# GELU on two hidden tiles at a time in a fused attention and MLP kernel

## The chip, the cores and the metric

The kernel runs on one core of a Trainium2 chip. The metric is device time in microseconds (us) of one execution; lower is better. Executions of the kernel before agree within 0.6% (421.8 to 424.2 us). Engines are named as in the profile: PE (matmul), PEld (its weight loads), DVE (vector), ACT (scalar), POOL, SP.

## The reference

Four layers are applied to x of 2048 rows by 512 columns, bf16: linear attention, MLP, attention, MLP, with the same weights twice. Cut to what matters:

```python
def _B_ref(x, w1, b1, w2, b2):                  # the MLP; F = 1792
    y = _layernorm(x, axis=-1)
    h = _gelu(jnp.einsum("bsd,df->bsf", y, w1) + b1)     # tanh form of GELU
    return jnp.einsum("bsf,fd->bsd", h, w2) + b2

x = x + _A_ref(_layernorm(x), A_wqkv, A_wo)     # linear attention, 32 heads of 16
x = x + _B_ref(_layernorm(x), B_w1, B_b1, B_w2, B_b2)
# ... and both once more
```

## The kernel before

All data stays on the core. Rows are worked in 4 chunks of 512. In an MLP layer PE makes h transposed, one tile of 128 hidden units by 512 rows at a time (4 matmuls, 14 tiles a chunk), and later y for each of 16 row tiles (15 matmuls; a y needs all 14 h tiles of its chunk). GELU of one h tile takes five instructions, on DVE and ACT in turn. A pipeline helper issues stage k of item i in step i+k, so that every engine has a fixed program order:

```python
for f in range(NF): H(0, f)                 # NF = 14
for c in range(1, NCH):
    ytiles = list(range(4 * (c - 1), 4 * c))
    for f in range(NF):
        H(c, f)
        if f in (5, 7, 9, 11) and ytiles:   # a y of the chunk before
            Y(ytiles.pop(0))
for t in range(4 * (NCH - 1), NT): Y(t)
# stages of an h item:
#  0 PE   4 matmuls into one of 8 PSUM banks
#  1 ACT (f % 3 == 1) or DVE: X = psum + b1        -> frees the bank
#  2 ACT  Q = Square(k * X)
#  3 DVE  P = (Q + c) * X                          (SCALAR_TENSOR_TENSOR, "STT")
#  4 ACT  S = Sigmoid(2 * P)
#  5 DVE  hT = S * X                               ("multiply")
# stages of a y item: 5 PE 15 matmuls; 8 DVE residual, then layer norm of the next layer is queued
_pipeline(items, 9, b_stage, per_step=lambda: K.drain(1))   # one queued piece of layer norm a step
```

PSUM banks are handed out in the order in which they were freed.

## Time and profile before

The median was 423.06 us in 6 runs.

| stage (from the trace of the kernel before) | us |
|---|---|
| first matmul | at 16.1 |
| attention, layer 1 | 87.1 |
| MLP, layer 2 | 118.6 |
| attention, layer 3 | 79.6 |
| MLP, layer 4, to the last matmul | 116.3 |

Each stage is counted from its own first matmul to the next stage's. First, groups of instructions of the kernel before: line, engine, operation, tiles, shapes and count; then busy time and mean ns of one; then idle time of the engine ahead of them, with what ended it.

```profile
L669 PE MATMUL ps<-lnT,w_sb 128*128 128x512 bf16 x448 | 108.3, 389 | 11.1 <-DVE st L681 8.3 <-ACT st L677 2.0 <-issue 0.6
L717 PE MATMUL ps<-w_sb,hT 128*128 128x512 bf16 x434 | 103.2, 387 | 7.0 <-ACT st L699 4.4 <-DVE hT L704 2.0
L693 DVE SCALAR_TENSOR_TENSOR st<-st 128x512 bf16<-128x512 bf16 x112 | 76.8, 686 | 6.7 <-ACT st L688 5.8
L699 ACT ACTIVATE st<-st 128x512 bf16<-128x512 bf16 x112 | 69.7, 622 | 17.4 <-DVE st L693 17.2
L681 DVE TENSOR_SCALAR st<-ps,b_f 128x512 bf16<-128x512 f32 x72 | 53.6, 745 | 7.2 <-PE ps L669 7.1
L704 DVE TENSOR_TENSOR hT<-st 128x512 bf16<-128x512 bf16 x112 | 45.7, 417 | 2.5 <-ACT st L699 2.5
L677 ACT ACTIVATE st<-ps,b_f 128x512 bf16<-128x512 f32 x40 | 26.8, 670 | 1.8 <-PE ps L669 1.8
```

L669 is h, L717 is y. PE waits 8.3 us in all for the DVE bias add (which frees its bank), and 4.4 + 2.0 us ahead of y for GELU results.

Next, windows of layer 2 in the same trace: a stretch of time, its length, busy us (and instructions) of PE, PEld, DVE, ACT, POOL, then the granted PE clock, the DMA share and GB/s.

```profile
112.00:116.00 4.00, 3.45 (x11) 1.20 (x12) 2.89 (x5) 3.63 (x5) 0.00 (x0) 0.72 0.70 131
124.00:128.00 4.00, 3.03 (x13) 0.95 (x12) 4.00 (x9) 3.81 (x8) 0.00 (x0) 1.00 0.02 4
128.00:132.00 4.00, 2.87 (x13) 0.86 (x11) 4.00 (x9) 3.78 (x8) 0.00 (x0) 1.00 0.00 0
132.00:136.00 4.00, 1.84 (x6) 0.68 (x6) 4.00 (x9) 3.90 (x8) 0.00 (x0) 0.78 0.00 0
136.00:140.00 4.00, 4.00 (x15) 1.49 (x14) 4.00 (x9) 3.54 (x7) 0.00 (x0) 0.79 0.00 0
160.00:172.00 12.00, 11.95 (x55) 5.04 (x55) 10.95 (x27) 8.39 (x16) 1.11 (x1) 1.00 0.23 44
```

Two regimes are seen. From 120 to 136 us DVE is always busy and PE is not: GELU sets the pace. From 160 us on PE is always busy: saving GELU time there buys nothing.

Last, PE's timeline in layer 2 of the same kernel (start, length, engine, line, operation, tiles, count, and in brackets the idle time before it and what ended it). First h, the last h before the first y, the first y, and the y of the last chunk:

```profile
103.12 7.07 PE L669 MATMUL ps<-lnT,w_sb 128*128 128x512 bf16 x32
131.62 1.02 PE L669 MATMUL ps<-lnT,w_sb 128*128 128x512 bf16 x4 [0.27 <-DVE st L681]
134.79 4.39 PE L717 MATMUL ps<-w_sb,hT 128*128 128x512 bf16 x13 [2.15 <-ACT st L699]
139.43 1.90 PE L669 MATMUL ps<-lnT,w_sb 128*128 128x512 bf16 x8
207.89 3.19 PE L717 MATMUL ps<-w_sb,hT 128*128 128x512 bf16 x14 [2.01 <-DVE hT L704]
```

The first y starts 31.7 us after the first h, and the y at 207.89 takes 3.19. (Some matmul records are missing from a trace, so 13 and 14 mean the same. Where it is the first of a y, the y seems to start about 0.2 us late and to take 2.97 us in place of 3.19; starts of a y are no better known than that.) The 2.01 us before the last chunk's y are a hole in the PE-bound part.

### The profile page before, as it was taken

The numbers are of one execution on the slowest core, as the hardware profiler recorded it, in microseconds if no ns is written. First come the engines' busy times: TensorE is split into PE (matmuls) and PEld (weight loads), VectorE is DVE, ScalarE is ACT, GpSimd is POOL, SyncE is SP. The second block draws the span as 40 slices with busy tenths as digits, with TensorE's granted clock in tenths as the row PEclk, the third lists the DMA queues.
The fourth block names the chain that finished last, engine by engine and source line by source line (L and its number), as shares of the span: only waits on it lengthen the run. The fifth ranks groups of instructions, "written<-read, shape, count | busy, mean of one in ns | idle before, by whom it ended". The sixth has DMA issues, their size and how long they took to land.

```text
span 420.4 us, 5871 instructions
## 1 busy us (share of the span) xinstructions
PE 363.6 (86%) x1921; PEld 164.4 (39%) x1952; DVE 338.7 (81%) x834; ACT 272.4 (65%) x524; POOL 24.9 (6%) x52
## 2 busy tenths in 40 slices
PE   0469997978776999999899999697887699999997
PEld 0124445544322444444344444654332244444442
DVE  4788776999699989999836877699879998987941
ACT  5536662545499896896727666255649987886820
POOL 6320000000100001000000000000100000000000
PEclk9989999899998999999999999899989899999999
DMA  8997000021600001102022000002250000010011
GB/s 295 205 295 156 2 0 2 2 51 30 120 2 0 0 2 24 27 2 50 2 50 50 2 0 0 2 3 51 51 100 2 1 12 27 12 39 12 26 39 37
DMA packets 40688, 18.74 MB, mean 45 GB/s; under 512 B 35473, under 2 KB 39570, under 8 KB 40658
## 3 DMA queue, kind: packets, MB, share of 16 engines
q1 hardware_dynamic: 39506, 12.59, 14.3%
q0 software_dynamic: 1152, 5.77, 4.1%
q8 instruction: 16, 0.26, 0.2%
q14 instruction: 14, 0.11, 0.1%
HBM read 7.87 MB, written 2.10 MB: 24 GB/s over the span
## 4 chain that ended last, share of the span: by engine, by line
issue 58%; PE 24%; DVE 8%; ACT 5%; POOL 4%; DMA 1%; POOLq 0%; DVEq 0%
PE ps L717 15%; PE ps L669 7%; POOL rs L364 3%; ACT st L688 2%; DVE st L388 2%; DVE st L693 2%; PE ps L719 2%; DVE st L681 1%; ACT st L699 1%; DVE ln_tok L375 1%; ACT st L677 1%; DMA x_sb<-in_A_x_dram 1%; DVE hT L704 1%; ACT st L338 1%; DVE x_sb L427 0%
## 5 line engine op out<-in xcount | busy, mean ns | idle before, releaser
L669 PE MATMUL ps<-lnT,w_sb 128*128 128x512 bf16 x448 | 108.3, 389 | 11.1 <-DVE st L681 8.3
L717 PE MATMUL ps<-w_sb,hT 128*128 128x512 bf16 x434 | 103.2, 387 | 7.0 <-ACT st L699 4.4
L693 DVE SCALAR_TENSOR_TENSOR st<-st 128x512 bf16<-128x512 bf16 x112 | 76.8, 686 | 6.7 <-ACT st L688 5.8
L688 ACT ACTIVATE st<-st 128x512 bf16<-128x512 bf16 x112 | 69.2, 623 | 19.5 <-DVE st L681 18.1
L699 ACT ACTIVATE st<-st 128x512 bf16<-128x512 bf16 x112 | 69.7, 622 | 17.4 <-DVE st L693 17.2
L669 PEld LDWEIGHTS ps<-lnT,w_sb 128*128 128x128 bf16 x448 | 40.9, 99 | 72.4 <-issue 13.0
L717 PEld LDWEIGHTS ps<-w_sb,hT 128*128 128x128 bf16 x448 | 43.8, 100 | 61.5 <-DVE hT L704 7.1
L475 PE MATMUL ps<-wqkv_sb,lnT 128*128 128x512 bf16 x249 | 57.3, 385 | 3.7 <-DVE pqT L509 3.4
L681 DVE TENSOR_SCALAR st<-ps,b_f 128x512 bf16<-128x512 f32 x72 | 53.6, 745 | 7.2 <-PE ps L669 7.1
L427 DVE SCALAR_TENSOR_TENSOR x_sb<-ps,x_sb 128x512 bf16<-128x512 f32 x64 | 43.3, 684 | 18.9 <-PE ps L719 18.3
L338 ACT ACTIVATE st<-x_sb 128x512 bf16<-128x512 bf16 x64 | 39.6, 620 | 20.9 <-DVE x_sb L427 15.4
L491 ACT ACTIVATE st<-ps 128x512 bf16<-128x512 f32 x64 | 37.8, 598 | 22.3 <-PE ps L475 9.2
L704 DVE TENSOR_TENSOR hT<-st 128x512 bf16<-128x512 bf16 x112 | 45.7, 417 | 2.5 <-ACT st L699 2.5
L462 PE MATMUL ps<-lnT,wqkv_sb 128*128 128x512 bf16 x128 | 31.7, 404 | 16.0 <-DMA lnT<-ln_tok 16.0
L598 ACT ACTIVATE oT<-ps 128x512 bf16<-128x512 bf16 x32 | 19.0, 593 | 39.5 <-PE ps L591 39.5
L475 PEld LDWEIGHTS ps<-wqkv_sb,lnT 128*128 128x128 bf16 x256 | 25.3, 99 | 34.8 <-DVE pqT L509 3.9
L609 PE MATMUL ps<-wo_sb,oT 128*128 128x512 bf16 x118 | 32.3, 388 | 4.8 <-DVE den_sb L573 2.9
L364 POOL TENSOR_TENSOR rs<-rs,neg_half 128x4 f32<-128x4 f32 x16 | 16.4, 1027 | 281.3 <-DVE rs L361 157.0
L375 DVE TENSOR_SCALAR ln_tok<-x_sb,mv,rs 128x512 bf16<-128x512 bf16 x64 | 22.7, 417 | 12.4 <-POOL rs L364 12.4
L677 ACT ACTIVATE st<-ps,b_f 128x512 bf16<-128x512 f32 x40 | 26.8, 670 | 1.8 <-PE ps L669 1.8
L497 DVE TENSOR_SCALAR st<-st 128x512 bf16<-128x512 bf16 x64 | 18.3, 287 | 11.0 <-ACT st L491 10.8
L462 PEld LDWEIGHTS ps<-lnT,wqkv_sb 128*128 128x128 bf16 x128 | 13.0, 103 | 33.0 <-issue 19.9
(55 smaller groups left out, 261.2 us busy)
## 6 DMA issues: line engine op xcount, KB each, us to landing
w_sb<-in_B_w_dram POOLq DMA_DIRECT2D x2, 1792.0 KB, 8.8
x_sb<-in_A_x_dram SPq DMA_DIRECT2D x4, 512.0 KB, 7.6
out_dram<-x_sb SPq DMA_DIRECT2D x16, 128.0 KB, 1.7
wqkv_sb<-in_A_wqkv_dram POOLq DMA_DIRECT2D x1, 1536.0 KB, 10.2
wo_sb<-in_A_wo_dram POOLq DMA_DIRECT2D x1, 512.0 KB, 4.7
lnT<-ln_tok SPq DMA_TRANSPOSE x16, 4.3
b_bf<-in_B_b_dram SPq DMA_DIRECT2D x1, 3.5 KB
biasblk<-in_B_b_dram SPq DMA_DIRECT2D x1, 1.0 KB
```

What stands on the lines that cost most here:

```text
L338: self.add(E_ACT, lambda e: e.activation(junk, x_t, ACT.Square, accum_out=self.ss[:, 1, t:t + 1]), reads=[("x", t)], writes=[("st", sJ), ( ...
L427: self.add(E_DVE, lambda e: e.scalar_tensor_tensor(out=x_t, in0=ps_ap, scalar=0.0, in1=x_t, op0=ALU.add, op1=ALU.add, accum_out=self.ss[:, ...
L462: ins = e.matmul(ps[:], K.wqkv_sb[:, gp, g * 128:(g + 1) * 128], K.lnT_ap(c)[:, :, gp, :], start=(gp == 0), stop=(gp == NG - 1))
L475: ins = e.matmul(ps[:], K.lnT_ap(c)[:, tl, gp, :], K.wqkv_sb[:, gp, col0:col0 + 512], start=(gp == 0), stop=(gp == NG - 1))
L491: K.add(E_ACT, lambda e: e.activation(stE, ps[:], ACT.Exp), reads=[("ps", it.b)], writes=[("st", it.sE)], name="phi_exp")
L669: ins = e.matmul(ps[:], K.w1_sb[:, gp, f * 128:(f + 1) * 128], K.lnT_ap(c)[:, :, gp, :], start=(gp == 0), stop=(gp == NG - 1))
L681: K.add(E_DVE, lambda e: e.tensor_scalar(stX, K.ps[it.b][:], K.b1_f[:, f:f + 1], None, op0=ALU.add), reads=[("ps", it.b), ("c", "b1f")], w ...
L688: K.add(E_ACT, lambda e: e.activation(stQ, stX, ACT.Square, scale=kq), reads=[("st", it.sX)], writes=[("st", it.sQ)], name="g_sq")
L693: K.add(E_DVE, lambda e: e.scalar_tensor_tensor(out=stP, in0=stQ, scalar=GELU_C, in1=stX, op0=ALU.add, op1=ALU.mult), reads=[("st", it.sQ) ...
L699: K.add(E_ACT, lambda e: e.activation(stS, stP, ACT.Sigmoid, scale=2.0), reads=[("st", it.sP)], writes=[("st", it.sS)], name="g_sig")
L704: K.add(E_DVE, lambda e: e.tensor_tensor(dest, stS, stX, ALU.mult), reads=[("st", it.sS), ("st", it.sX)], writes=[("hT", slot, f)], name=" ...
L717: ins = e.matmul(ps[:], K.hT[:, slot, f, tl * 128:(tl + 1) * 128], K.w2_sb[:, f, :], start=(f == 0), stop=False)
```

## The change

The intent is to pay the fixed cost of each GELU instruction once for two h tiles. An h item is now a pair; Square, STT, Sigmoid and multiply are 1024 wide; the bias add stays 512 wide (its bias differs and each tile has its own bank), one half on DVE and the other on ACT. Staging buffers come from a free list so that two neighbours can be had. The y items stand after pairs 3, 4, 5, 6 of a chunk. Cut to its core:

```diff
-        for f in range(NF):
-            H(0, f)
+        for j in range(NPAIR):
+            H(0, j)
         for c in range(1, NCH):
             ytiles = list(range(4 * (c - 1), 4 * c))
-            for f in range(NF):
-                H(c, f)
-                if f in (5, 7, 9, 11) and ytiles:
+            for j in range(NPAIR):
+                H(c, j)
+                if j in (3, 4, 5, 6) and ytiles:
                     Y(ytiles.pop(0))
 ...
                 elif k == 1:
-                    if f % 3 == 1:   # ACT ... else DVE
+                    it.sX = K.alloc_st(2)
+                    stX = K.st2ap(it.sX)
+                    K.add(E_DVE, ... tensor_scalar(stX[:, 0:512], K.ps[it.bA][:], b1 of f0 ...), name="g_x")
+                    K.add(E_ACT, ... activation(stX[:, 512:1024], K.ps[it.bB][:], ACT.Identity, b1 of f0+1 ...), name="g_xa")
 ...
                 elif k == 2:
-                    stX, stQ = K.st[:, it.sX, :], K.st[:, it.sQ, :]
+                    stX, stQ = K.st2ap(it.sX), K.st2ap(it.sQ)      # 1024 wide
                     K.add(E_ACT, lambda e: e.activation(stQ, stX, ACT.Square, scale=kq), ...)
 ...   # stages 3, 4, 5 in the same way
```

The rest of the diff (own junk buffers for the layer norm sums, four den buffers instead of 16, one constant sharing another's buffer, an unused option to normalize on ACT) does no different work.

More of the change, by code (lines that the diff above doesn't have):

```diff
@@ L21 @@
 DEBUG_INST_MAP = {}
+TEST_SEP_IDENT = False
 GELU_C = math.sqrt(2.0 / math.pi)
@@ L157, in __init__ @@
         self.sems = {}
-        self.rr_st = 0
         self.free_banks = deque(range(8))
@@ L177, in release_bank, with alloc_st, release_st, st1 @@
         self.free_banks.append(b)
-    def next_st(self):
-        s = self.rr_st
-        self.rr_st = (self.rr_st + 1) % self.NST
-        return s
+    def alloc_st(self, n=1):
+        free = self.st_free
+        if n == 1:
+            u = free.popleft()
+            return u
+        for u in list(free):
+            if u % 2 == 0 and (u + 1) in free:
+                free.remove(u)
+                free.remove(u + 1)
+                return u
+        raise AssertionError("staging pool: no free pair (restructure the pipeline)")
+    def release_st(self, u, n=1):
+        for k in range(n):
+            assert (u + k) not in self.st_free
+            self.st_free.append(u + k)
+    def st1(self, u):
+        return self.st[:, u, :]
+    def st2ap(self, u):
+        return self.st[:, u:u + 2, :].rearrange("p a k -> p (a k)")
     def dump(self, name, src_ap, reads):
@@ L203, in alloc @@
         nc, P, NT, NG, NF, S, D = self.nc, self.P, self.NT, self.NG, self.NF, self.S, self.D
-        self.NST = 24
+        self.NST = 26
         self.NLN = 8
@@ L220, in alloc @@
         self.st = self.sb("st", [P, self.NST, 512], BF16)
+        self.st_free = deque(range(self.NST))
+        self.junk_act = self.sb("junk_act", [P, 2, 512], BF16)
+        self.junk_dve = self.sb("junk_dve", [P, 2, 512], BF16)
         self.wqkv_sb = self.sb("wqkv_sb", [P, NG, 3 * D], BF16)
@@ L230, in alloc @@
         self.rs = self.sb("rs", [P, 2, NT], F32)
-        self.den_sb = self.sb("den_sb", [P, NT, 32], F32)
-        self.rden = self.sb("rden", [P, NT, 32], F32)
+        self.nmr = self.sb("nmr", [P, NT], F32)
+        self.NDS = 4
+        self.den_sb = self.sb("den_sb", [P, self.NDS, 32], F32)
+        self.rden = self.sb("rden", [P, self.NDS, 32], F32)
         self.z_sb = self.sb("z_sb", [P, NG], F32)
@@ L236, in alloc @@
         self.neg_half = self.sb("neg_half", [P, 1], F32)
+        self.eps_col = self.sb("eps_col", [P, 1], F32)
         self.maskf = self.sb("maskf", [P, 128], F32)
@@ L239, in alloc @@
         self.mask8f = self.sb("mask8f", [P, 8], F32)
-        self.identf = self.sb("identf", [P, 128], F32)
+        self.identf = self.sb("identf", [P, 128], F32) if TEST_SEP_IDENT else self.maskf
         self.ident = self.sb("ident", [P, 128], BF16)
@@ L296, in build_consts @@
         self.add(E_DVE, lambda e: e.memset(self.neg_half[:], -0.5), writes=[("c", "neg_half")], name="c_neghalf")
+        self.add(E_DVE, lambda e: e.memset(self.eps_col[:], 1e-6), writes=[("c", "eps")], name="c_eps")
         for t in range(self.NT):
@@ L312, in build_consts @@
                  reads=[("c", "maskf")], writes=[("c", "mask16")], name="c_mask16")
-        self.add(E_POOL, lambda e: e.memset(self.identf[:], 1.0), writes=[("c", "identf")], name="c_id0")
+        self.add(E_POOL, lambda e: e.memset(self.identf[:], 1.0), reads=[("c", "mask16")],
+                 writes=[("c", "identf"), ("c", "maskf")], name="c_id0")
         self.add(E_POOL, lambda e: e.affine_select(self.identf[:], self.identf[:], [[1, 128]], ALU.is_equal, 0.0,
@@ L325, in build_consts @@
                  reads=[("c", "mask8f")], writes=[("c", "mask8f")], name="c_mask8c")
-    def ln_sum_tile(self, t):
-        x_t = self.x_sb[:, t, :]
-        sJ = self.next_st()
-        junk = self.st[:, sJ, :]
-        self.add(E_ACT, lambda e: e.activation(junk, x_t, ACT.Identity, accum_out=self.ss[:, 0, t:t + 1]),
-                 reads=[("x", t)], writes=[("st", sJ), ("ss0", t)], name=f"sum{t}")
     def ln_sumsq_tile(self, t):
         x_t = self.x_sb[:, t, :]
-        sJ = self.next_st()
-        junk = self.st[:, sJ, :]
+        junk = self.junk_act[:, t % 2, :]
         self.add(E_ACT, lambda e: e.activation(junk, x_t, ACT.Square, accum_out=self.ss[:, 1, t:t + 1]),
-                 reads=[("x", t)], writes=[("st", sJ), ("ss1", t)], name=f"sumsq{t}")
+                 reads=[("x", t)], writes=[("junk_act", t % 2), ("ss1", t)], name=f"sumsq{t}")
     def ln_chunk_stats(self, c, double):
@@ L365, in ln_chunk_stats, with ln_chunk_norm @@
                  reads=[("rs0", c), ("c", "neg_half")], writes=[("rs", c)], name=f"rstd{c}")
-    def ln_chunk_norm(self, c, lngroup):
+    def ln_chunk_norm(self, c, lngroup, act_tiles=0):
         P = self.P
@@ L370, in ln_chunk_norm @@
         s0 = (c % 2) * 4
+        if act_tiles:
+            nmr4 = self.nmr[:, t0:t0 + 4]
+            self.add(E_DVE, lambda e: e.scalar_tensor_tensor(out=nmr4, in0=self.mv[:, t0:t0 + 4, 0], scalar=-1.0,
+                                                             in1=self.rs[:, 1, t0:t0 + 4], op0=ALU.mult,
+                                                             op1=ALU.mult),
+                     reads=[("mv", t) for t in range(t0, t0 + 4)] + [("rs", c)], writes=[("nmr", c)], name=f"nmr{c}")
         for i in range(4):
@@ L374, in ln_chunk_norm @@
             dst = self.ln_tok[:, s0 + i, :]
-            self.add(E_DVE, lambda e, dst=dst, x_t=x_t, t=t: e.tensor_scalar(
-                dst, x_t, self.mv[:, t, 0:1], self.rs[:, 1, t:t + 1], op0=ALU.subtract, op1=ALU.mult),
-                reads=[("x", t), ("mv", t), ("rs", c)], writes=[("lnk", s0 + i)], name=f"norm{t}")
+            if i < act_tiles:
+                self.add(E_ACT, lambda e, dst=dst, x_t=x_t, t=t: e.activation(
+                    dst, x_t, ACT.Identity, bias=self.nmr[:, t:t + 1], scale=self.rs[:, 1, t:t + 1]),
+                    reads=[("x", t), ("nmr", c), ("rs", c)], writes=[("lnk", s0 + i)], name=f"norma{t}")
+            else:
+                self.add(E_DVE, lambda e, dst=dst, x_t=x_t, t=t: e.tensor_scalar(
+                    dst, x_t, self.mv[:, t, 0:1], self.rs[:, 1, t:t + 1], op0=ALU.subtract, op1=ALU.mult),
+                    reads=[("x", t), ("mv", t), ("rs", c)], writes=[("lnk", s0 + i)], name=f"norm{t}")
         src = self.ln_tok[:, s0:s0 + 4, :]
@@ L385, in ln_sum_tile_dve @@
         x_t = self.x_sb[:, t, :]
-        sJ = self.next_st()
-        junk = self.st[:, sJ, :]
+        junk = self.junk_dve[:, t % 2, :]
         self.add(E_DVE, lambda e: e.tensor_scalar(junk, x_t, 1.0, 0.0, op0=ALU.mult, op1=ALU.add,
                                                   accum_out=self.ss[:, 0, t:t + 1]),
-                 reads=[("x", t)], writes=[("st", sJ), ("ss0", t)], name=f"sumd{t}")
+                 reads=[("x", t)], writes=[("junk_dve", t % 2), ("ss0", t)], name=f"sumd{t}")
     def emit_ln_layer0(self):
@@ L398, in emit_ln_layer0 @@
             self.ln_chunk_norm(c, self.ln_groups[0][c])
-            if c == 1:
+            last = self.NCH - 1
+            if c == min(1, last):
                 self.load_wo()
-            if c == 2:
+            if c == min(2, last):
                 self.load_w1()
-            if c == 3:
+            if c == min(3, last):
                 self.load_w2()
@@ L422, in post_residual @@
             self.defer(lambda c=c, nl=nl: self.ln_chunk_stats(c, self.layer_kinds[nl] == "B"))
-            self.defer(lambda c=c, nl=nl: self.ln_chunk_norm(c, self.ln_groups[nl][c]))
+            self.defer(lambda c=c, nl=nl: self.ln_chunk_norm(c, self.ln_groups[nl][c],
+                                                                 act_tiles=(0 if self.layer_kinds[nl] == "B" else 0)))
     def residual(self, t, bank_res, ps_ap, name):
@@ L488, in a1_stage @@
                 else:
-                    it.sE = K.next_st()
-                    stE = K.st[:, it.sE, :]
+                    it.sE = K.alloc_st()
+                    stE = K.st1(it.sE)
                     K.add(E_ACT, lambda e: e.activation(stE, ps[:], ACT.Exp), reads=[("ps", it.b)],
@@ L494, in a1_stage @@
                 if it.kind != "v":
-                    it.sE1 = K.next_st()
-                    stE, stE1 = K.st[:, it.sE, :], K.st[:, it.sE1, :]
+                    it.sE1 = K.alloc_st()
+                    stE, stE1 = K.st1(it.sE), K.st1(it.sE1)
                     K.add(E_DVE, lambda e: e.tensor_scalar(stE1, stE, 1.0, 1e-6, op0=ALU.min, op1=ALU.add),
                           reads=[("st", it.sE)], writes=[("st", it.sE1)], name="phi_e1")
+                    K.release_st(it.sE)
             elif k == 3:
@@ L501, in a1_stage @@
                     ps = K.ps[it.b]
-                    stE1 = K.st[:, it.sE1, :]
+                    stE1 = K.st1(it.sE1)
                     if it.kind == "q":
@@ L512, in a1_stage @@
                     K.release_bank(it.b)
+                    K.release_st(it.sE1)
         _pipeline(items, 4, a1_stage, per_step=lambda: K.drain(1))
@@ L571, in a3_stage @@
                 den_ps = K.ps[it.bt][:, 0:32]
-                dsb, rd = K.den_sb[:, t, :], K.rden[:, t, :]
+                ds = t % K.NDS
+                dsb, rd = K.den_sb[:, ds, :], K.rden[:, ds, :]
                 K.add(E_DVE, lambda e: e.tensor_scalar(dsb, den_ps, 1e-6, None, op0=ALU.add),
-                      reads=[("ps", it.bt)], writes=[("den", t)], name=f"dene{t}")
-                K.add(E_DVE, lambda e: e.reciprocal(rd, dsb), reads=[("den", t)], writes=[("rden", t)],
+                      reads=[("ps", it.bt)], writes=[("den", ds)], name=f"dene{t}")
+                K.add(E_DVE, lambda e: e.reciprocal(rd, dsb), reads=[("den", ds)], writes=[("rden", ds)],
                       name=f"rden{t}")
@@ L581, in a3_stage @@
                     rd.unsqueeze(2).to_broadcast([P, 32, 16]), ALU.mult),
-                    reads=[("ps", it.b), ("rden", t)], writes=[("otk", it.slot)], name=f"o{t}")
+                    reads=[("ps", it.b), ("rden", ds)], writes=[("otk", it.slot)], name=f"o{t}")
                 K.release_bank(it.b)
@@ L628, in layer_B @@
         kq = math.sqrt(GELU_C * GELU_A)
+        assert NF % 2 == 0
+        NPAIR = NF // 2
         class It:
@@ L633, in layer_B, with H @@
         items = []
-        def H(c, f):
+        def H(c, j):
             it = It()
-            it.kind, it.c, it.f = "h", c, f
+            it.kind, it.c, it.f0 = "h", c, 2 * j
             items.append(it)
@@ L656, in layer_B, with hgroup, fn @@
             Y(t)
+        def hgroup(ps, c, f):
+            def fn(e):
+                ins = None
+                for gp in range(NG):
+                    ins = e.matmul(ps[:], K.w1_sb[:, gp, f * 128:(f + 1) * 128],
+                                   K.lnT_ap(c)[:, :, gp, :], start=(gp == 0), stop=(gp == NG - 1))
+                return ins
+            return fn
         def b_stage(it, k):
             if it.kind == "h":
-                c, f = it.c, it.f
+                c, f0 = it.c, it.f0
@@ L661, in b_stage @@
                 slot = c % 2
                 if k == 0:
-                    it.b = K.alloc_bank()
-                    ps = K.ps[it.b]
-                    def fn(e):
-                        ins = None
-                        for gp in range(NG):
-                            ins = e.matmul(ps[:], K.w1_sb[:, gp, f * 128:(f + 1) * 128],
-                                           K.lnT_ap(c)[:, :, gp, :], start=(gp == 0), stop=(gp == NG - 1))
-                        return ins
-                    K.add(E_PE, fn, reads=[("w", "w1")] + K.lnT_res(c), writes=[("ps", it.b)], name=f"h{c}_{f}")
-                elif k == 1:
-                    it.sX = K.next_st()
-                    stX = K.st[:, it.sX, :]
-                    if f % 3 == 1:
-                        K.add(E_ACT, lambda e: e.activation(stX, K.ps[it.b][:], ACT.Identity,
-                                                            bias=K.b1_f[:, f:f + 1], scale=1.0),
-                              reads=[("ps", it.b), ("c", "b1f")], writes=[("st", it.sX)], name="g_xa")
-                    else:
-                        K.add(E_DVE, lambda e: e.tensor_scalar(stX, K.ps[it.b][:], K.b1_f[:, f:f + 1], None,
-                                                           op0=ALU.add),
-                              reads=[("ps", it.b), ("c", "b1f")], writes=[("st", it.sX)], name="g_x")
-                    K.release_bank(it.b)
@@ new lines, in b_stage @@
+                    it.bA = K.alloc_bank()
+                    it.bB = K.alloc_bank()
+                    K.add(E_PE, hgroup(K.ps[it.bA], c, f0), reads=[("w", "w1")] + K.lnT_res(c),
+                          writes=[("ps", it.bA)], name=f"h{c}_{f0}")
+                    K.add(E_PE, hgroup(K.ps[it.bB], c, f0 + 1), reads=[("w", "w1")] + K.lnT_res(c),
+                          writes=[("ps", it.bB)], name=f"h{c}_{f0 + 1}")
+                elif k == 1:
+                    it.sX = K.alloc_st(2)
+                    stX = K.st2ap(it.sX)
+                    K.add(E_DVE, lambda e: e.tensor_scalar(stX[:, 0:512], K.ps[it.bA][:], K.b1_f[:, f0:f0 + 1], None,
+                                                       op0=ALU.add),
+                          reads=[("ps", it.bA), ("c", "b1f")], writes=[("st", it.sX)], name="g_x")
+                    K.release_bank(it.bA)
+                    K.add(E_ACT, lambda e: e.activation(stX[:, 512:1024], K.ps[it.bB][:], ACT.Identity,
+                                                        bias=K.b1_f[:, f0 + 1:f0 + 2], scale=1.0),
+                          reads=[("ps", it.bB), ("c", "b1f")], writes=[("st", it.sX + 1)], name="g_xa")
+                    K.release_bank(it.bB)
@@ L685, in b_stage @@
                 elif k == 2:
-                    it.sQ = K.next_st()
-                    stX, stQ = K.st[:, it.sX, :], K.st[:, it.sQ, :]
+                    it.sQ = K.alloc_st(2)
+                    stX, stQ = K.st2ap(it.sX), K.st2ap(it.sQ)
                     K.add(E_ACT, lambda e: e.activation(stQ, stX, ACT.Square, scale=kq),
-                          reads=[("st", it.sX)], writes=[("st", it.sQ)], name="g_sq")
+                          reads=[("st", it.sX), ("st", it.sX + 1)],
+                          writes=[("st", it.sQ), ("st", it.sQ + 1)], name="g_sq")
@@ L690, in b_stage @@
                 elif k == 3:
-                    it.sP = K.next_st()
-                    stX, stQ, stP = K.st[:, it.sX, :], K.st[:, it.sQ, :], K.st[:, it.sP, :]
+                    it.sP = K.alloc_st(2)
+                    stX, stQ, stP = K.st2ap(it.sX), K.st2ap(it.sQ), K.st2ap(it.sP)
                     K.add(E_DVE, lambda e: e.scalar_tensor_tensor(out=stP, in0=stQ, scalar=GELU_C, in1=stX,
                                                                   op0=ALU.add, op1=ALU.mult),
-                          reads=[("st", it.sQ), ("st", it.sX)], writes=[("st", it.sP)], name="g_p")
+                          reads=[("st", it.sQ), ("st", it.sQ + 1), ("st", it.sX), ("st", it.sX + 1)],
+                          writes=[("st", it.sP), ("st", it.sP + 1)], name="g_p")
@@ L696, in b_stage @@
+                    K.release_st(it.sQ, 2)
                 elif k == 4:
-                    it.sS = K.next_st()
-                    stP, stS = K.st[:, it.sP, :], K.st[:, it.sS, :]
+                    it.sS = K.alloc_st(2)
+                    stP, stS = K.st2ap(it.sP), K.st2ap(it.sS)
                     K.add(E_ACT, lambda e: e.activation(stS, stP, ACT.Sigmoid, scale=2.0),
-                          reads=[("st", it.sP)], writes=[("st", it.sS)], name="g_sig")
+                          reads=[("st", it.sP), ("st", it.sP + 1)],
+                          writes=[("st", it.sS), ("st", it.sS + 1)], name="g_sig")
@@ L701, in b_stage @@
+                    K.release_st(it.sP, 2)
                 elif k == 5:
-                    stX, stS = K.st[:, it.sX, :], K.st[:, it.sS, :]
-                    dest = K.hT[:, slot, f, :]
+                    stX, stS = K.st2ap(it.sX), K.st2ap(it.sS)
+                    dest = K.hT[:, slot, f0:f0 + 2, :].rearrange("p f k -> p (f k)")
                     K.add(E_DVE, lambda e: e.tensor_tensor(dest, stS, stX, ALU.mult),
-                          reads=[("st", it.sS), ("st", it.sX)], writes=[("hT", slot, f)], name="g_out")
+                          reads=[("st", it.sS), ("st", it.sS + 1), ("st", it.sX), ("st", it.sX + 1)],
+                          writes=[("hT", slot, f0), ("hT", slot, f0 + 1)], name="g_out")
@@ L706, in b_stage @@
+                    K.release_st(it.sS, 2)
+                    K.release_st(it.sX, 2)
             else:
```

## The prediction

> **What bounds it now.** The page gives PE 86%, DVE 81%, ACT 65%. Windows over the two MLP layers show two regimes. (1) Start of the layer: in the timeline the first h matmul of layer 2 runs at 103.1 us, the first y matmul at 134.8 us. From 120 to 136 us DVE is busy 4.00 of every 4 us and ACT about 3.8, PE only 1.8 to 3.0: PE waits for PSUM banks that the bias add frees. Layer 4 repeats it (301 to 333 us). PE idles 8.5 us there in layer 2. (2) From the first y on, PE is busy 11.95 of 12 us, DVE about 11, ACT 8.4 to 11.4: PE-bound, so GELU work saved there is worth nothing. One hole remains: 2.0 us at 205.9 us in layer 2, where y of the last chunk waits for the last GELU output on DVE. Layer 4 has none.
>
> **What the change does.** GELU works on two 512-wide tiles at once: 56 wide Squares, Sigmoids, STTs and multiplies in place of 112 each; bias adds split evenly (DVE 72 to 56, ACT 40 to 56). The first y moves from after 23 h tiles in PE's order to after 26. The rest should cost nothing.
>
> **Costs.** Mean durations overstate: instructions on one engine overlap. In the saturated stretch starts are 0.60 us apart after an STT, 0.66 after a bias add, 0.335 after the multiply; on ACT 0.52 for Square or Sigmoid, 0.58 for the bias add. So three tiles cost DVE 2x0.66+3x0.60+3x0.335 = 4.13 us (seen: 4.12), ACT 3.7: DVE-bound, 1.37 us a tile. The Trainium skill (ScalarE: Activation LUTs, what a table load costs) gives 0.833 ns an element and 93 ns overlap of back-to-back ACTIVATEs; 622 ns against 0.52 us here agrees with the overlap. No instruction here is 1024 wide, so as an estimate: Square or Sigmoid 0.52+0.43 = 0.95 us (duration about 1.05), STT 1.13 (duration about 1.22), multiply 0.60 (duration about 0.68). A pair then costs DVE 0.66+1.13+0.60 = 2.40 us, ACT 0.58+2x0.95 = 2.48: ACT-bound, 1.24 us a tile. Only 0.07 to 0.1 us per merged instruction is saved.
>
> **On the critical path.** Replaying ACT's order from the first bias add (111.5 us, one table load of 1.28 us included), the first y starts near 133.5 to 134.5 us instead of 134.8, with 26 h tiles done instead of 23 (0.87 us each): 2 to 4 us a layer, say 3.3. The 2.0 us hole goes, since three y (9.6 us) now follow the last h on PE. Sum: 2x3.3+2.0 = 8.6 us; I take 1 us off for new small waits of coarser steps (banks taken two at a time).
>
> Predicted: 415.5 us, range 410 to 420.5. Faster by over 2%: 0.40; within 2%: 0.56; slower: 0.04.
>
> **What would show it.** Right: wide Square and Sigmoid about 1.05 us, STT 1.22, multiply 0.68; ACT full from about 120 us to the first y; first y near 134 us after 26 h tiles; no hole near 206 us; PE still above 98% busy after the first y; attention layers unchanged within 1 us. Wrong: first y later than 136 us, or PE holes in the y stretch behind bias adds or multiplies.
>
> **What would make it wrong.** A pair's longer latency could delay the first y. The granted PE clock falls to 0.6 to 0.8 near 112, 134, 312 and 332 us, after waits; other gaps could move each by about 1 us. If wide instructions save their full fixed part, the gain passes 2%.

## More of the kernel before

Between attention and MLP, `self.drain()` issues all that is left of the layer norm queue before the first MLP instruction.

## The result

The changed kernel took 414.89 us (median of 8 runs, 414.20 to 415.51), the kernel before 423.21 us. The ratio is 0.9805, with a 95% interval of 0.979 to 0.982. (A ratio is the mean time of one kernel's runs over that of the other's runs of the same rounds, so not quite the ratio of the medians.) That is 8.3 us less; the interval contains 0.98, so whether it is a full 2% is unclear.

The groups of the changed kernel, columns as before (L697 h, L764 y, L733 STT, L741 Sigmoid, L727 Square, L716 and L720 bias adds, L748 multiply):

```profile
L697 PE MATMUL ps<-lnT,w_sb 128*128 128x512 bf16 x448 | 104.1, 380 | 10.0 <-DVE st L716 7.2 <-ACT st L720 2.3
L764 PE MATMUL ps<-w_sb,hT 128*128 128x512 bf16 x434 | 99.7, 379 | 5.9 <-DVE st L716 2.8 <-DVE hT L748 2.6
L733 DVE SCALAR_TENSOR_TENSOR st<-st 128x1024 bf16<-128x1024 bf16 x56 | 68.4, 1222 | 5.3 <-ACT st L727 5.1
L741 ACT ACTIVATE st<-st 128x1024 bf16<-128x1024 bf16 x56 | 59.3, 1058 | 20.5 <-DVE st L733 19.9
L727 ACT ACTIVATE st<-st 128x1024 bf16<-128x1024 bf16 x56 | 58.9, 1051 | 5.4 <-DVE st L716 4.9
L716 DVE TENSOR_SCALAR st<-ps,b_f 128x512 bf16<-128x512 f32 x56 | 41.3, 745 | 2.5 <-PE ps L697 2.4
L748 DVE TENSOR_TENSOR hT<-st 128x1024 bf16<-128x1024 bf16 x56 | 38.0, 686 | 13.2 <-PE ps L766 8.0 <-ACT st L741 5.2
```

The wide durations are those predicted (1.05, 1.22, 0.68 us). PE's total wait is hardly smaller: 10.0 and 5.9 us against 11.1 and 7.0. But its busy time fell too, by 4.2 us for h and 3.5 us for y, with the same matmuls. That is a change of PE's clock, and the windows of layer 2 show it:

```profile
124.00:128.00 4.00, 3.26 (x13) 0.94 (x12) 4.00 (x6) 4.00 (x6) 0.00 (x0) 1.00 0.01 2
128.00:132.00 4.00, 3.52 (x14) 1.15 (x15) 4.00 (x5) 4.00 (x6) 0.00 (x0) 1.00 0.02 4
132.00:136.00 4.00, 2.68 (x11) 0.73 (x9) 3.95 (x7) 4.00 (x6) 0.00 (x0) 1.00 0.00 0
136.00:140.00 4.00, 3.53 (x16) 1.59 (x18) 3.77 (x6) 4.00 (x6) 0.00 (x0) 1.00 0.00 0
160.00:172.00 12.00, 11.95 (x54) 5.08 (x54) 10.71 (x21) 9.21 (x14) 1.01 (x1) 1.00 0.00 0
```

ACT is now the engine without a pause, and the clock stays at 1.00. PE's timeline in layer 2 of the changed kernel:

```profile
105.36 7.07 PE L697 MATMUL ps<-lnT,w_sb 128*128 128x512 bf16 x32
133.01 2.07 PE L697 MATMUL ps<-lnT,w_sb 128*128 128x512 bf16 x8 [0.40 <-DVE st L716]
136.47 2.97 PE L764 MATMUL ps<-w_sb,hT 128*128 128x512 bf16 x13 [1.39 <-DVE hT L748]
139.69 1.90 PE L697 MATMUL ps<-lnT,w_sb 128*128 128x512 bf16 x8
149.73 2.97 PE L764 MATMUL ps<-w_sb,hT 128*128 128x512 bf16 x13 [1.24 <-DVE st L716]
208.12 3.20 PE L764 MATMUL ps<-w_sb,hT 128*128 128x512 bf16 x14
```

The first y starts 31.1 us after the first h (31.7 before), with 26 h tiles done instead of 23. It runs at full clock. The hole before the last chunk's y is gone. A new wait of 1.24 us stands before the third y (1.55 us in layer 4).

These five terms account for the two MLP layers. An h tile costs PE 0.865 us (four tiles lie between 152.95 and 156.41 us). The time from the start of the first y to the h after it was 4.64 us, now 3.22 us in layer 2 (4.72 and 3.22 in layer 4).

| term, us | layer 2 | layer 4 |
|---|---|---|
| three more h tiles done before the first y | -2.6 | -2.6 |
| first y earlier after the first h | -0.6 | -0.6 |
| first y at full clock | -1.4 | -1.5 |
| hole before the last chunk's y | -2.0 | 0 |
| new wait before the third y | +1.2 | +1.5 |
| sum | -5.4 | -3.2 |
| measured change of the stage (118.55 to 113.09; 116.28 to 113.03) | -5.5 | -3.3 |

Layer 3 changed by 0.2 us. Layer 1 took 89.5 us in this trace and 87.1 in that of before; a second trace of the kernel before showed 89.8, so I take this as variation between runs. (Hence the two profiled runs, 422.18 and 415.48 us, differ by 6.7 us only, though the MLP layers alone give 8.7.)

### The profile page after: what moved, and what is told of

Same layout as the page of the kernel before. It is cut to its first block, busy times and chain, and to the rows that moved or that the text cites. A ratio compares the mean times of both kernels' runs of the same rounds, so it can differ in the third digit from the quotient of the medians. Undisturbed runs are those within 1.5% of the kernel's fastest.

```text
span 413.8 us, 5708 instructions
## 1 busy us (share of the span) xinstructions
PE 358.1 (87%) x1921; PEld 162.8 (39%) x1952; DVE 321.7 (78%) x707; ACT 263.5 (64%) x428; POOL 24.7 (6%) x52
## 4 chain that ended last, share of the span: by engine, by line
PE 44%; issue 26%; DVE 17%; ACT 9%; POOL 2%; DMA 1%; POOLq 0%; DVEq 0%; ACTq 0%
PE ps L764 21%; PE ps L697 10%; PE ps L505 6%; ACT st L727 4%; DVE st L733 3%; PE ps L492 3%; ACT st L741 2%; DVE o_tok L612 2%; PE ps L766 2%; ACT st L720 2%; POOL rs L382 2%; DVE x_sb L457 2%; DVE ln_tok L404 2%; DVE st L716 2%; DVE hT L748 1%
## 5 line engine op out<-in xcount | busy, mean ns | idle before, releaser
L697 PE MATMUL ps<-lnT,w_sb 128*128 128x512 bf16 x448 | 104.1, 380 | 10.0 <-DVE st L716 7.2
L764 PE MATMUL ps<-w_sb,hT 128*128 128x512 bf16 x434 | 99.7, 379 | 5.9 <-DVE st L716 2.8
L733 DVE SCALAR_TENSOR_TENSOR st<-st 128x1024 bf16<-128x1024 bf16 x56 | 68.4, 1222 | 5.3 <-ACT st L727 5.1
L741 ACT ACTIVATE st<-st 128x1024 bf16<-128x1024 bf16 x56 | 59.3, 1058 | 20.5 <-DVE st L733 19.9
L697 PEld LDWEIGHTS ps<-lnT,w_sb 128*128 128x128 bf16 x448 | 40.5, 97 | 68.6 <-issue 8.3
L764 PEld LDWEIGHTS ps<-w_sb,hT 128*128 128x128 bf16 x448 | 42.6, 98 | 58.2 <-issue 4.3
L505 PE MATMUL ps<-wqkv_sb,lnT 128*128 128x512 bf16 x249 | 58.7, 391 | 4.8 <-DVE pqT L540 4.5
L727 ACT ACTIVATE st<-st 128x1024 bf16<-128x1024 bf16 x56 | 58.9, 1051 | 5.4 <-DVE st L716 4.9
L356 ACT ACTIVATE junk_act<-x_sb 128x512 bf16<-128x512 bf16 x64 | 39.6, 620 | 20.4 <-DVE x_sb L457 10.9
L748 DVE TENSOR_TENSOR hT<-st 128x1024 bf16<-128x1024 bf16 x56 | 38.0, 686 | 13.2 <-PE ps L766 8.0
L631 ACT ACTIVATE oT<-ps 128x512 bf16<-128x512 bf16 x32 | 19.0, 594 | 39.8 <-PE ps L624 39.7
L720 ACT ACTIVATE st<-ps,b_f 128x512 bf16<-128x512 f32 x56 | 38.0, 679 | 9.8 <-DVE b_f L658 4.9
L716 DVE TENSOR_SCALAR st<-ps,b_f 128x512 bf16<-128x512 f32 x56 | 41.3, 745 | 2.5 <-PE ps L697 2.4
L492 PEld LDWEIGHTS ps<-lnT,wqkv_sb 128*128 128x128 bf16 x128 | 13.0, 103 | 32.8 <-DMA lnT<-ln_tok 15.8
```

Source lines behind the costliest of these rows:

```text
L356: self.add(E_ACT, lambda e: e.activation(junk, x_t, ACT.Square, accum_out=self.ss[:, 1, t:t + 1]), reads=[("x", t)], writes=[("junk_act", ...
L492: ins = e.matmul(ps[:], K.wqkv_sb[:, gp, g * 128:(g + 1) * 128], K.lnT_ap(c)[:, :, gp, :], start=(gp == 0), stop=(gp == NG - 1))
L505: ins = e.matmul(ps[:], K.lnT_ap(c)[:, tl, gp, :], K.wqkv_sb[:, gp, col0:col0 + 512], start=(gp == 0), stop=(gp == NG - 1))
L697: ins = e.matmul(ps[:], K.w1_sb[:, gp, f * 128:(f + 1) * 128], K.lnT_ap(c)[:, :, gp, :], start=(gp == 0), stop=(gp == NG - 1))
L716: K.add(E_DVE, lambda e: e.tensor_scalar(stX[:, 0:512], K.ps[it.bA][:], K.b1_f[:, f0:f0 + 1], None, op0=ALU.add), reads=[("ps", it.bA), (" ...
L720: K.add(E_ACT, lambda e: e.activation(stX[:, 512:1024], K.ps[it.bB][:], ACT.Identity, bias=K.b1_f[:, f0 + 1:f0 + 2], scale=1.0), reads=[(" ...
```

## The experiments

The open question was which part of the change pays: the width, the even split of the bias adds, or the new order of h and y, and whether the clock is a cause or a by-product. All 12 kernels gave correct results. They ran in three groups of four, each beside runs of the kernel before on the same chip, whose medians were 422.68 us (n_both, n_act, n_dve, b_ylate), 422.86 us (b_warm, a_yearly, b_both, a_nodrain) and 422.51 us (before2, b_warm2, b_nodrain, a_nd_act). "Start" below means the time from the first h to the first y of a layer.

### Width taken away

The changed kernel with its pairs, its order and its split, but each wide instruction issued as two:

```diff
-                    K.add(E_ACT, lambda e: e.activation(stQ, stX, ACT.Square, scale=kq), ...
+                    for u in range(2):
+                        K.add(E_ACT, lambda e, u=u: e.activation(stQ[:, 512*u:512*u+512],
+                                                                 stX[:, 512*u:512*u+512], ACT.Square, scale=kq), ...
   # likewise Sigmoid, STT and multiply
```

> The changed kernel with its order, its pairs and its even split of the bias adds, but each wide instruction issued as two of 512. Theory (in the start of the layer the busier engine sets the pace, and width saves only the fixed part): ACT then needs 4x0.52+0.58 = 2.66 us a pair instead of the 2.46 seen after the change; over the some 13 to 16 pairs until the GELU-bound stretch ends that is 2 to 3 us a layer, so 419 to 420 us (ratio 0.991). Rival 1, order and split do it all: 415 us (0.981). Rival 2, width does it all: 423 us (1.00).

Measured: 416.10 us, ratio 0.9847 (0.9833 to 0.9860). My theory was wrong here: I expected 419 to 420. Without any wide instruction 6.6 of the 8.3 us stay. The MLP stages were 114.0 and 113.8 us, so width is worth 0.9 + 0.8 = 1.7 us.

The engine rates were as computed for ACT (2.65 us a pair), but the bias adds on DVE came every 2.53 us, not every 2.65. DVE's timeline of this run; start to start of L716 is the pace:

```profile
128.49 0.74 DVE L716 TENSOR_SCALAR st<-ps,b_f 128x512 bf16<-128x512 f32 x1
129.15 0.75 DVE L752 TENSOR_TENSOR hT<-st 128x512 bf16<-128x512 bf16 x2
129.82 1.28 DVE L735 SCALAR_TENSOR_TENSOR st<-st 128x512 bf16<-128x512 bf16 x2
131.03 0.74 DVE L716 TENSOR_SCALAR st<-ps,b_f 128x512 bf16<-128x512 f32 x1
```

DVE does not wait for ACT in these lines. ACT (2.65 us) falls behind by about 0.1 us a pair, which the buffers between them can take for the some ten pairs that count. I read this from the two engines' start times; no run varied the number of pairs.

### Half of the width

Square and Sigmoid narrow, DVE wide (the two ACT edits above alone):

> The changed kernel with Square and Sigmoid narrow, DVE wide. Theory: ACT is the pacing engine of the start (2.66 us a pair against DVE 2.40), so nearly all that width gives is lost: 419 us, within 1 us of the fully narrow one. Rival, the width of the DVE instructions matters as much: half way, about 417 us.

Measured: 419.86 us, ratio 0.9925 (0.9911 to 0.9938). The number is as expected, but for another reason than the one given, since the fully narrow kernel is 3.8 us faster: a wide DVE instruction behind two narrow ACT instructions must wait for the second of them (in the trace DVE idles 0.17 to 0.35 us before most wide STT of the start, until the second Square has ended). The bias adds now come every 2.66 us, and the third y waits 1.88 us, 0.9 us more than in the fully narrow kernel. Wide on DVE alone is worse than not wide at all; the MLP stages show 2.5 of the 3.8 us.

STT and multiply narrow, ACT wide (the two DVE edits alone):

> The changed kernel with STT and multiply narrow, ACT wide. Theory: DVE then needs 0.66+2x0.60+2x0.335 = 2.53 us a pair, just above ACT's 2.46: 0.07 us a pair, about 1 us a layer, so 416 to 417 us. Rival, every instruction saved on DVE counts with its full fixed part of 0.15 us: 112 instructions fewer are lost, well over 419 us.

Measured: 415.61 us, ratio 0.9831 (0.9818 to 0.9844), within 0.7 us of the changed kernel. The pace was 2.53 us a pair, the number worked out. How the 1.7 us of width divides is not settled: by the stages of the traces 1.3 us come from ACT and 0.5 from DVE, by the ratios (0.9847, 0.9831, 0.9805) 0.7 and 1.1, and neighbouring intervals overlap. Shown is only that ACT alone can be wide without loss, and DVE alone can't.

### Order alone

The kernel before, all narrow, only the y items moved by two h tiles:

```diff
-                if f in (5, 7, 9, 11) and ytiles:
+                if f in (7, 9, 11, 13) and ytiles:
```

> The kernel before with only the y tiles moved two h tiles later in the order (after h 7, 9, 11, 13 of a chunk), all instructions narrow, old split. Theory: the hole of 2.0 us at the end of layer 2 goes, since two y follow the last h, and the first y comes after 25 h tiles instead of 23, worth 0.7 to 1 us a layer: about 419.5 us (0.992). Rival (width does it all): 423 us.

Measured: 417.14 us, ratio 0.9866 (0.9853 to 0.9879). One line of order gives 5.5 of the 8.3 us, 2.4 us more than I expected. PE at the first y of layer 2 of this run:

```profile
135.79 1.02 PE L669 MATMUL ps<-lnT,w_sb 128*128 128x512 bf16 x4 [0.23 <-DVE st L681]
137.56 2.97 PE L717 MATMUL ps<-w_sb,hT 128*128 128x512 bf16 x13 [0.74 <-issue]
140.77 1.90 PE L669 MATMUL ps<-lnT,w_sb 128*128 128x512 bf16 x8
```

The wait before the first y is 0.74 us instead of 2.15, and the clock does not fall. The first y comes 0.9 us later than before (32.6 us after the first h) but with two more tiles done (-1.7 us), at full clock (-1.4), and the hole of 2.0 us is gone: together -4.2 us; the stage went from 118.55 to 114.22. In layer 4 the first y ran at full clock too (-1.5). These 2.9 us of clock stood in no expectation of mine, and they are about the 2.4 us by which the run beat it.

With the even split of the bias adds on top (`f % 2 == 1` in place of `f % 3 == 1`), no pairs:

> The kernel before with the y tiles two h tiles later and the bias adds split evenly, all narrow, no pairs. Theory: a tile then costs ACT 1.33 us and DVE 1.27 instead of DVE 1.37, 0.04 us a tile over some 18 tiles: 0.7 us a layer better than the later y alone (417.1): about 416 us, the same as pairs of narrow instructions. Rival (pairing by itself helps): as the later y alone, 417 us.

Measured: 418.44 us, ratio 0.9898 (0.9881 to 0.9915): no gain, rather a loss. A pair of tiles took 2.65 us as computed (2.75 with the later y alone), yet the first y started 32.8 us after the first h, not earlier. The MLP stages differ by only 0.6 us in all from those of the later y alone. Why the better pace brought nothing is not tested, but the traces give a likely cause. With the even split the bias add of the fourth tile falls to ACT and runs behind an ACT_TABLE_LOAD of 1.28 us, which precedes the first Sigmoid: in layer 2 at 117.64 us, 13.5 us after the first h, where DVE did it 11.5 us after in the kernel with the later y alone. In the fully narrow pairs above it came before the table load, 10.1 us after the first h. That order is the likely gain of pairs as such; no run here tests it.

### The order of y, the other way

The changed kernel with each y one pair earlier:

```diff
-                if j in (3, 4, 5, 6) and ytiles:
+                if j in (2, 3, 4, 5) and ytiles:
```

> The changed kernel with every y one pair earlier in the order (after pairs 2, 3, 4, 5), so that 24 h tiles stand before the first y instead of 26. Theory (order and clock carry most of the gain): PE's wait before the first y grows from 1.3 to over 3 us, the clock falls there, the first y takes over 4 us, the holes of 1.2 to 1.6 us before the third y shrink: 1.5 us a layer are lost, about 418 us (0.988). Rival (width carries the gain): 415 us as the changed kernel.

Measured: 418.55 us, ratio 0.9901 (0.9878 to 0.9924), as expected. About half of the gain, 4.0 of 8.3 us, is lost with every wide instruction in place. The first y of layer 2 and the window behind it:

```profile
135.97 4.88 PE L764 MATMUL ps<-w_sb,hT 128*128 128x512 bf16 x14 [3.41 <-DVE hT L748]
```

```profile
132.00:136.00 4.00, 0.59 (x4) 0.10 (x3) 4.00 (x7) 4.00 (x6) 0.00 (x0) 1.00 0.00 0
136.00:140.00 4.00, 4.00 (x12) 1.46 (x13) 3.52 (x4) 4.00 (x6) 0.00 (x0) 0.64 0.00 0
```

A wait of 3.41 us, then a clock of 0.64 and a y of 4.88 us. Two tiles fewer (+1.7), the first y 0.5 us earlier, the low clock (+1.9, from 135.97 to the next h at 141.10), and no wait before the third y (-1.2) make +1.9 us; the stage grew by 2.0. (The record of a first matmul may shift 0.2 us between two of these terms.) The six runs ranged from 417.35 us at a mean clock of 0.984 to 420.31 us at 0.971. The times of this kernel move with the mean granted clock. Those of the kernel before do not: beside these experiments its nine runs at a mean clock of 0.971 or 0.972 took 422.2 to 422.7 us, and six at 0.980 took 422.9 to 423.5. So the mean clock alone does not tell the time.

### The clock by itself

A second trace of the kernel before, unchanged:

> The kernel before, unchanged, for a second trace of it. Theory (a wait of PE of about 2 us can, but need not, drop its clock; which wait it hits changes from run to run): y starts where it did (31.3 to 31.7 us after the first h), but the set of cold stretches may differ. Rival (the dip before the first y is a fixed property of this kernel): the same four dips as in the first trace.

Measured: 423.64 us (a single run). The first y of layers 2 and 4 ran at a low clock again: 0.57 and 0.58 in one 4 us window each, 4.66 us in place of 3.2. The dips near 112 and 312 us of the first trace were absent, and the time was not better for it. So of the four dips in the first trace two recurred, and those stood directly ahead of PE-bound work. PE in layer 2 of this second trace:

```profile
135.87 4.66 PE L717 MATMUL ps<-w_sb,hT 128*128 128x512 bf16 x13 [1.98 <-DVE hT L704]
140.77 1.90 PE L669 MATMUL ps<-lnT,w_sb 128*128 128x512 bf16 x8
209.30 3.20 PE L717 MATMUL ps<-w_sb,hT 128*128 128x512 bf16 x14 [2.08 <-DVE hT L704]
```

A wait of 2.08 us later in the same layer was followed by a y at full speed. Ahead of it PE had been busy all the time; ahead of the first y it had been busy for about 3 of every 4 us. But that is no rule: in a later run (the kernel before without the forced emptying, below) waits of 2.01 and 1.98 us before the first y left the clock at 1.00. The Trainium skill (TensorE: Matmul & The Clock Gate, section What's actually happening) says that the clock follows PE's activity in a window that runs on by itself. That agrees with dips that come and go from run to run; what decides one dip, no run here shows.

To take the low clock away and nothing else, PE was given matmuls on data that was ready, in the bank of that y, which overwrites them. The first attempt:

```diff
+                    if t == 0:
+                        # nine matmuls of w1 and a ready chunk into ps, start=True on the first
+                        K.add(E_PE, warm, reads=[("w", "w1")] + K.lnT_res(1), writes=[("ps", it.b)], name="warm")
                     K.add(E_PE, fn, ...)        # the y itself
```

> The kernel before, plus nine extra matmuls on data that is ready, issued by PE into the PSUM bank of the first y of each MLP layer just ahead of that y (which then overwrites it), to fill the 2.15 and 2.23 us in which PE waits there; all else, the moment at which the last GELU output is ready included, is unchanged. Theory (part of the change's gain is that PE's clock no longer falls after that wait): the granted clock around the first y stays near 1.00 instead of 0.78, the first y takes 3.2 us in place of 4.4, so 1.2 us a layer are gained although PE does more work: 420.4 us against 422.8 (0.9945). Rival (the clock has nothing to do with the gain): no change or up to 1 us slower.

Measured: 424.15 us, ratio 1.0023 (1.0006 to 1.0041): a miss. The trace shows why. The first y of both layers did run at full clock, and layer 4 was 1.0 us shorter. But in layer 2 the wait before the last chunk's y remained, and now the clock fell there:

```profile
137.09 3.18 PE L717 MATMUL ps<-w_sb,hT 128*128 128x512 bf16 x14
209.05 4.82 PE L717 MATMUL ps<-w_sb,hT 128*128 128x512 bf16 x14 [2.07 <-DVE hT L704]
```

That y took 1.6 us longer than its like in the kernel before, after a wait of the same length. One of the six runs took 422.14 us at a mean clock of 0.984; the other five took 424.1 to 424.4 us at 0.976.

Second attempt: eight such matmuls at the first y of both layers and also before the last chunk's y of layer 2.

> The kernel before with eight extra matmuls on ready data in front of the first y of both MLP layers and in front of the first y of the last chunk of layer 2, so that none of the three waits of 2.0 to 2.2 us leaves PE idle (in the earlier attempt the last of them stayed, and the y behind it ran at the low clock: 4.82 us in place of 3.19). Theory (low clock after these waits costs 1.2 to 1.6 us each): all y take 3.2 us, 420.5 us against 422.8 (0.9945). Rival (no direct cost of the clock): 422.8 us or more.

Measured: 421.41 us, ratio 0.9964 (0.9950 to 0.9979). No y was slow. PE did more work and the kernel took about 1.1 us less, half of what I expected. The first y took 3.22 us up to the next h (137.24 to 140.46) instead of 4.64 and 4.90, but it started 32.1 and 31.7 us after the first h, 0.4 us later than in the first trace and 0.7 to 0.8 us later than in the second:

```profile
137.24 2.97 PE L717 MATMUL ps<-w_sb,hT 128*128 128x512 bf16 x13 [0.36 <-PE ps L725]
```

The MLP stages were 1.0 and 1.1 us shorter, as these two terms give. So a low clock costs time by itself; the inserted work gave part of it back.

### A version that beats both

In the changed kernel the first bias add of layer 2 runs on DVE at 113.6 us, 8.3 us after the first h. DVE stands before two waits for POOL there (1.19 and 1.12 us idle), because the forced emptying of the layer norm queue puts layer norm of chunks 2 and 3 ahead of all GELU. The helper would issue these pieces one a step anyway, and chunk 2 is not needed before pair 14.

```diff
         _pipeline(tiles, 6, a3_stage, per_step=lambda: K.drain(1))
-        self.drain()
```

> The changed kernel without the forced emptying of the layer norm queue between attention and MLP: the layer norm of chunks 2 and 3 is issued one piece a step among the first GELU steps, so that DVE no longer stands still behind two waits for POOL (1.19 and 1.12 us) before the first bias add. Theory (GELU on DVE and ACT bounds the first 45 us of the layer): the first bias add starts some 5 us earlier, DVE's own work stays, its idle 2 to 3 us a layer are gained: about 410 us (0.969). Rival (PE order alone bounds the start): 415 us.

Measured: 408.51 us, ratio 0.9660 (0.9645 to 0.9675), the fastest kernel. DVE of this run around the first bias adds (L715):

```profile
107.03 0.17 DVE L379 TENSOR_SCALAR rs<-mv 128x4 f32<-128x4 f32 x1
107.11 0.74 DVE L715 TENSOR_SCALAR st<-ps,b_f 128x512 bf16<-128x512 f32 x1
108.32 1.38 DVE L404 TENSOR_SCALAR ln_tok<-x_sb,mv,rs 128x512 bf16<-128x512 bf16 x4 [0.47 <-POOL rs L382]
109.62 0.74 DVE L715 TENSOR_SCALAR st<-ps,b_f 128x512 bf16<-128x512 f32 x1
```

The first bias add stands 2.4 us after the first h (104.73 us), in the middle of POOL's work. The first y starts after 28.5 us instead of 31.1, and each MLP stage is about 3 us shorter (110.0 us both). This confirms that GELU, and not PE's order alone, bounds the start.

The same line taken from the kernel before:

> The kernel before without the forced emptying of the layer norm queue between attention and MLP, nothing else. Theory (start of the layer is bound by GELU, and this fills DVE's idle time there whatever the width): 3 us a layer, as the changed kernel gained (414.9 to 408.5): about 416.5 us (0.985), so the change and this add up. Rival (the old order of y gives the earlier start back as a longer wait of PE before the last chunk's y or the first y): under 3 us in all.

Measured: 416.46 us, ratio 0.9848 (0.9831 to 0.9865), as expected. The hole before the last chunk's y is still there (2.07 us), and this gain and the change's add up: 0.9848 x 0.9805 = 0.966. But the number is as expected in part by luck. In the profiled run each MLP stage is 3.9 us shorter, of which the earlier first y gives only 2.6 and 2.4 us; the other 1.4 and 1.5 us are the clock, which stayed at 1.00 behind this wait:

```profile
134.23 2.97 PE L716 MATMUL ps<-w_sb,hT 128*128 128x512 bf16 x13 [2.01 <-ACT st L698]
```

The last run tried to relieve DVE in attention, where it was busy 11.5 of 12 us, by giving ACT the eight normalizations of chunks 0 and 1:

```diff
-    act_tiles=(0 if self.layer_kinds[nl] == "B" else 0)
+    act_tiles=(4 if self.layer_kinds[nl] == "B" and c < 2 else 0)
```

> The changed kernel without the forced emptying, and the layer norm of chunks 0 and 1 before each MLP layer done by ACT instead of DVE (8 tiles a layer, 0.34 us of DVE each). Theory (the second half of attention is DVE-bound: 11.5 of 12 us busy, ACT 6): 2.4 us a layer less, about 404.5 us (0.957). Rival (there the chain from bank to bank sets the pace, not DVE's work): 408.5 us.

Measured: 418.40 us (416.79 to 420.60), ratio 0.9903: 10 us worse than without it. ACT and PE of this run, in attention of layer 1:

```profile
89.92 2.92 ACT L400 ACTIVATE ln_tok<-x_sb,nmr,rs 128x512 bf16<-128x512 bf16 x4 [3.25 <-DVE nmr L391]
92.75 0.57 ACT L631 ACTIVATE oT<-ps 128x512 bf16<-128x512 bf16 x1
93.42 1.86 PE L642 MATMUL ps<-wo_sb,oT 128*128 128x512 bf16 x4 [2.78 <-DVE rden L608]
```

ACT waits 3.25 us in program order for the statistics, then does four normalizations in a row, and only then the eviction (L631) that PE needs; PE stands for 2.78 us, and the clock fell to 0.57 in the window from 92 to 100 us. (The line names L608 of DVE as the releaser, but that had ended at 92.80 us; the matmul reads oT, which L631 had written by 93.32.) The two attention layers grew by 6.5 and 5.6 us, the MLP layers did not. The engine with time to spare was the wrong place for work that has to wait.

## Why the prediction was right

The prediction was 415.5 us with a range of 410 to 420.5; 414.89 us was measured, on the edge between "within 2%" (0.56) and "faster" (0.40). Point by point:

- The regimes were right: GELU-bound up to the first y, PE-bound after, but for one wait a layer (below). The version without the forced emptying confirms the first: an earlier GELU start shortens each MLP layer by 3 us.
- The estimate of wide durations was right: 1.05 and 1.06 us for Square and Sigmoid, 1.22 for STT, 0.69 for multiply. The slope of the Trainium skill (ScalarE: Activation LUTs, section What ACT_TABLE_LOAD costs), 0.833 ns an element, agrees with this trace: 512 more elements took 428 to 436 ns. Bias adds came every 2.46 us a pair; 2.48 was predicted.
- "First y near 134 us after 26 h tiles" was right: 31.1 us after the first h, which is 134.2 us in the time of the trace before. The absolute 136.5 us comes from a layer 1 that was 2.5 us longer in that run. The start gave 3.2 us a layer (3.3 predicted), the hole 2.0 us (2.0 predicted).
- "I take 1 us off for new small waits" was too small. The waits before the third y took 1.24 and 1.55 us, 2.8 us in all. The trace names the DVE bias add, which frees a bank: the sort of wait that was meant, at nearly three times the size. The prediction had listed PE holes behind bias adds as a sign that it was wrong; one came in each layer.
- The clock was named only as a risk of about 1 us each way and stood in no sum. It gave 1.4 and 1.5 us. These two misses, 1.8 us too few for waits and 2.9 us not counted for the clock, largely cancel. That the total of 8.6 - 1 = 7.6 us came out so near the 8.3 us measured is partly luck.
- What the prediction did not say is which part of the change earns the gain. It reads as if wide instructions did. The runs put 5.5 us on moving y by two h tiles, with every instruction narrow (2.9 us of it by the clock at the first y), and 1.7 us on width. Pairs, the even split and the 26th tile are left with about 1 us, which the runs do not divide further.
- "Attention layers unchanged within 1 us" held for layer 3 (79.6 and 79.4 us) and can't be judged for layer 1, which varied from 87.1 to 89.8 us between two traces of the same kernel.

## What to carry to other kernels

Where engines run fixed programs, look at what the slowest consumer stands behind before making instructions cheaper: here one line of order gave three times what the width of the GELU instructions gave, and one line that took a forced emptying away gave another 6 us. When several instructions are merged, try both engines of a chain: here wide instructions on the engine that sets the pace did no harm alone, and those on the other engine alone lost 3.8 us, because they waited for the narrow side. Count PE's clock as a possible cost of a wait: 2 us without work could make the y that followed 1.4 to 1.7 us longer.

## What the Trainium skill lacked or had wrong

- TensorE: Matmul & The Clock Gate (section HAM oscillation) gives the rule of no PE gap above about 3.4 us. Here waits of 1.98 to 2.23 us before the first y were followed by a granted clock of 0.57 to 0.80 (means over 4 us) in both traces of the kernel before, while waits of 2.01 and 2.08 us in a fully busy stretch were not; in one run a wait of 2.07 us in such a stretch was. Waits of 2.01 and 1.98 us before the first y of one more kernel left the clock at 1.00. So the rule misses gaps well below 3.4 us, which can cost 1.4 to 1.7 us each, in some runs and not in others. The same page (section A second HAM failure mode) does describe frequent short idles between groups of matmuls that let the clock swing; what it lacks is their length.
- VectorE: DVE Perf Modes gives durations and slopes, but no size for how much instructions that follow each other overlap. Durations of 686, 745 and 417 ns went with starts 600, 660 and 335 ns apart in the kernel before. So merging two STT saved 0.06 us of DVE time (1.14 against 1.20 us), and two multiplies 0.07 (0.60 against 0.67 where nothing else held up the next start), not the fixed part of a duration. The skill has such a figure on another page, Vector Engine (DVE) Microarchitecture Reference (section Measured stream behaviour on trn2): about 75 ns an instruction after overlap, near what was saved here.
- No page has the effect of merging on one side of a two-engine chain: 419.86 us with DVE wide and ACT narrow, 415.61 with ACT wide and DVE narrow, 416.10 with both narrow, 414.89 with both wide.
